# Scores and maxima of a grouped attention in 32-row TensorE tiles, four heads at a time

## The chip, the cores and the metric

The kernel runs on one core of a Trainium2 chip. The metric is device time in microseconds of one execution. Before the change three executions took 1123.99, 1124.51 and 1124.54; the median is 1124.51. A profile is one more execution, recorded instruction by instruction.

The engines that matter: TensorE (PE in the profile; its weight loads are shown as PEld), VectorE (DVE), ScalarE (ACT), GpSimd (POOL), and SyncE (SP), from whose queue nearly all DMAs are issued. Each engine works through its own instructions in the written order.

## The reference

One layer norm feeds two branches, and both are added to the input:

```python
xn = _layernorm(x)                        # x: 1 x 2048 x 448
# A: 16 heads of 28, one shared k and v
q = (xn @ wq) split into 16 heads; k = xn @ wk; v = xn @ wv      # 28 wide
p = softmax(q k^T * 28**-0.5, over the 2048 keys)
a = concat_heads(p v) @ wo
# B: a dense MLP
h = max(xn @ w1, 0)                       # 448 -> 1792
return x + a + h @ w2                     # 1792 -> 448
```

All data is float32.

## The kernel before, in words

**Precision.** A float32 value is split into a high part (rounded to the format float32r, which TensorE streams in one pass) and a low part, the rest. A product is then hi x hi + hi x lo + lo x hi; the scores also take lo x lo. Plain float32 matmuls, used for PV, appear in the profile as two instructions each.

**Stages.** The projection stage normalizes and transposes x in four blocks of 512 rows (`transposed`), projects q, k and v (`qkv_proj`, `qkv_first`), splits the result into both parts and writes it to a scratch in DRAM, `qscr` (`qkv_out`, L237). Then `kst` is read back (L309): a stack of 4 x 28 = 112 rows with the k parts, so that one matmul over 112 rows makes all four products of the parts. The MLP follows: 7 parts of the hidden width x 4 row blocks = 28 tasks, each with two up tiles (`mlp_up`, `proj`, 11 matmuls each, L168 and L173) and four down tiles (`mlp_down`, 6 matmuls each, L404). Last comes attention, in 16 units (4 query blocks of 512 x 4 groups of 4 heads).

**Maxima.** A softmax needs the maximum over the keys per query first. `max_tile` (L350, L354) multiplies 128 queries of one head by 512 keys and reduces the result on VectorE; 64 such tiles make a unit, 1024 in all. 192 of them run in the MLP's last 16 tasks, one between a few MLP matmuls (`LEAD, PER = 192, 12`), the other 832 in attention. `max_rows` transposes a unit's maxima (L371) and writes them by DMA into two more rows of the unit's query stack `qst`, against two rows of ones in `kst`: a score matmul over 114 rows so yields score minus maximum.

**Attention.** `score` (L628) multiplies one key block of 128 keys by 512 queries of one head and takes the exponential on ScalarE (L630). `pv` (L474) adds four heads' p by v into one PSUM bank: each head writes 32 of the 128 output rows, so four matmuls sit side by side in four column strips of TensorE. A column of ones in `vtile` gives the sums for the division. `dens`, `recips` and `normalized` divide, partly by way of DRAM; `o_proj` (L529) multiplies by wo, 12 matmuls for 128 rows; `o_proj_part` and `finish` deal with the last units.

**Order.** The order of the attention stage is written out in a string, one letter an instruction: `S` or `s` a score (PSUM pool A or M), `M` a maximum, `F` an output projection, `Vn` the PV of the oldest n key blocks. It holds 1024 scores, 832 maxima, 15 projections and 80 V groups of two to five blocks. A stretch of it:

```python
        7SM MS 2SM S V2 SSM 2MS 5SM MS 2SM S V4 2SM SSM 4MS SMMS 5SM S V4 S 3SM 2MS 5SM S V3 2SM SSM 3MS
```

PSUM has eight banks: pool A three, pool M four, pool O one. SP's queue holds, in the written order, the q writes, the loads of k and v and of the query stacks, the maxima's rows and the division's small transfers.

Of the kernel before, what the change touches and what calls it, by code (L numbers as in the profile page):

```python
# [15 lines left out]

@with_exitstack
def attention_plus_mlp(ctx: ExitStack, tc: tile.TileContext, x, wq, wk, wv, wo, w1, w2, out):
# [6 lines left out]
    NT = S // P  # L29
    QB = 512  # L30
    NQB = S // QB
    TPB = QB // P
    HG = 4
    NHG = H // HG
    NKB = S // P
# [4 lines left out]
    NPART = DFF // FP  # L40
# [5 lines left out]
    KQ = 4 * DH  # L46
    NU = NQB * NHG
    NA, NM = 3, 4
    assert DR == 64 and KQ + 2 <= P and HG * 32 == P and NPART * FP == DFF

# [4 lines left out]
    psA = ctx.enter_context(tc.tile_pool(name="psA", bufs=NA, space=PSUM))  # L55
    psM = ctx.enter_context(tc.tile_pool(name="psM", bufs=NM, space=PSUM))
    psO = ctx.enter_context(tc.tile_pool(name="psO", bufs=1, space=PSUM))

# [3 lines left out]
    for t in range(TPB):  # L62
        (nc.scalar if t % 2 else nc.sync).dma_start(acc[:, t, :], xv[:, t, :])

    ident = cst.tile([P, P], F32, name="ident")
    make_identity(nc, ident)
    vtile = cst.tile([P, NKB, 32], F32, name="vtile")
    nc.gpsimd.memset(vtile, 1.0)
    ones2 = cst.tile([2, QB], F32, name="ones2")
    nc.gpsimd.memset(ones2, 1.0)  # L70
    eps_t = cst.tile([P, 1], F32, name="eps_t")
    nc.vector.memset(eps_t, EPS)
    warm = cst.tile([P, 1], F32, name="warm")

# [3 lines left out]
    kst = cst.tile([P, S], F32R, name="kst")  # L78
    qscr = dram.tile([NHG, 2, P, S], F32, name="qscr")
    rscr = dram.tile([NU, HG, QB], F32, name="rscr")  # L80
    stacks = ctx.enter_context(tc.tile_pool(name="stacks", bufs=3))


    mlp = ExitStack()
    spool = mlp.enter_context(tc.tile_pool(name="spool", bufs=2))
    wpool = mlp.enter_context(tc.tile_pool(name="wpool", bufs=2))
    xpool = mlp.enter_context(tc.tile_pool(name="xpool", bufs=1))
    hpool = mlp.enter_context(tc.tile_pool(name="hpool", bufs=2))
    proj_scope = ExitStack()
    npool = proj_scope.enter_context(tc.tile_pool(name="npool", bufs=1, side="right"))  # L90
# [13 lines left out]
    DHH = DH // 2  # L104
    MQ = HG * DH
# [7 lines left out]
    wqkv = wpool.tile([P, 2, 4, 512], F32R, name="w")  # L113
    w4 = wqkv.rearrange("p s c (g n) -> p s c g n", g=NHG)
    nc.gpsimd.memset(w4[:, :, :, :, MQ + DHH : P].bitcast(F32), 0.0)
# [3 lines left out]
    def wqkv_parts(c, kv):  # L119
        src = (kvs if kv else s3)[:, c].rearrange("p (g n) -> p g n", g=NHG)  # L120
        cols = slice(MQ, MQ + DHH) if kv else slice(0, MQ)
        return src, w4[:, 0, c, :, cols], w4[:, 1, c, :, cols]
# [32 lines left out]
    xH = xpool.tile([P, DC, S], F32R, name="xH")  # L155
    xL = xpool.tile([P, DC, S], F32R, name="xL")
    xR = xpool.tile([P, S], F32R, name="xR")
    kstF = kst.bitcast(F32)

    def proj(ps, lhs, cols, xs, between=None, middle=None):  # L160

        n = 0
        for ws, xm in (((0, 1), xH), ((0,), xL)):
            if middle and xm is xL:
                middle()
            for c in range(DC):
                for wi in ws:
                    nc.tensor.matmul(ps, lhs[:, wi, c, cols], xm[:, c, xs], start=n == 0, stop=False)  # L168
                    n += 1
                    if between and n % 4 == 0:  # L170
                        between()
        for wi in range(2):
            nc.tensor.matmul(ps, lhs[:, wi, DC, cols], xR[:, xs], start=False, stop=wi == 1)  # L173
# [12 lines left out]

# [12 lines left out]

# [17 lines left out]
    def transposed(b, xn, chunks=range(DC + 1), order=range(TPB)):  # L217
        xs = slice(b * QB, (b + 1) * QB)
        for c in chunks:
# [3 lines left out]
            if c < DC:  # L223
                nc.scalar.activation(xH[:, c, xs], pt, AF.Copy)
                nc.vector.tensor_tensor(xL[:, c, xs], pt, xH[:, c, xs].bitcast(F32), op=ALU.subtract)
            else:
                tmp = small.tile([P, QB], F32R, name="tmp")
                nc.scalar.activation(xR[0:DR, xs], pt[0:DR], AF.Copy)
                nc.scalar.activation(tmp[DR:P], pt[DR:P], AF.Copy)
                nc.vector.tensor_tensor(xR[DR:P, xs], pt[DR:P], tmp[DR:P].bitcast(F32), op=ALU.subtract)  # L230
# [7 lines left out]

    def qkv_proj(b, g, spare=False, middle=None):
        pq = psO.tile([P, QB], F32, name="o") if spare else psA.tile([P, QB], F32, name="a")  # L240
        proj(pq, wqkv, slice(g * P, (g + 1) * P), slice(b * QB, (b + 1) * QB), middle=middle)
        return pq

    def qkv_first(gs):

        pq = [psA.tile([P, QB], F32, name="a") for _ in gs]
        passes = [(0, xH, c) for c in range(DC)] + [(0, xL, c) for c in range(DC)] + [(0, None, DC)]
        passes += [(1, xH, c) for c in range(DC)] + [(1, None, DC)]
        for n, (wi, xm, c) in enumerate(passes):
            for k, g in enumerate(gs):  # L250
                rhs = xR[:, 0:QB] if xm is None else xm[:, c, 0:QB]
                nc.tensor.matmul(  # L252
                    pq[k], wqkv[:, wi, c, g * P : (g + 1) * P], rhs, start=n == 0, stop=n == len(passes) - 1
                )
        return pq

# [18 lines left out]


# [8 lines left out]
    qkv_out(0, 3, pq)  # L285
    for b in range(1, NQB):
# [15 lines left out]
    proj_scope.close()  # L302
    stacks2 = ctx.enter_context(tc.tile_pool(name="stacks2", bufs=2, side="right"))


    for g in range(2):
        for r in range(4):
            d0 = r * DH + g * DHH
            nc.sync.dma_start(kstF[d0 : d0 + DHH, :], qscr[g, r // 2, MQ : MQ + DHH])  # L309
    for b in range(NQB):  # L310
        nc.sync.dma_start(kstF[KQ : KQ + 2, b * QB : (b + 1) * QB], ones2)
    vT = []
    for s in range(2):
        t = stacks.tile([P, HG, QB], F32, name="qst")
        vT.append(t.rearrange("d j q -> d (j q)")[0:DH])
        for g in range(2):
            nc.sync.dma_start(vT[s][g * DHH : (g + 1) * DHH], qscr[2 + g, s, MQ : MQ + DHH])
    nc.gpsimd.tensor_tensor(vT[0], vT[0], vT[1], op=ALU.add)

    def v_rows():  # L320

        pv = psM.tile([P, QB], F32, name="m")
        for kb in range(NKB):
            nc.tensor.transpose(pv[:, kb * 32 : kb * 32 + DH], vT[0][:, kb * P : (kb + 1) * P], ident[0:DH, 0:DH])
        nc.vector.tensor_copy(vtile[:, :, 0:DH], pv.rearrange("p (i d) -> p i d", d=32)[:, :, 0:DH])


    qst, nmx, mx_todo = {}, {}, []
    units = [(b, g) for b in range(NQB) for g in range(NHG)]

    def load_stack(u):
        if u >= NU:
# [355 lines left out]
```

## Time and profile before

| what | value |
|---|---|
| median of 3 executions | 1124.51 us (1123.99 to 1124.54) |
| the profiled execution: span, first to last instruction | 1122.0 us |
| its own time | not recorded beside the span; the median is 2.5 us above the span |
| projections, MLP, attention with its ending | 59.1, 321.8, 741.1 us |
| matmul instructions | 5900 |

A row of a group names the line, the engine, the operation, output and inputs with their shapes and the count; then the busy time of all of them in microseconds and the mean of one in nanoseconds; then how long the engine had been idle just before them, and what ended that. Matmuls overlap, so the mean of one is longer than the distance between two. In a row in order of time the first number is the start and the second the length, of one instruction or of a run of like ones ("x16"). In a stretch (A:B) each engine's busy time is followed by its number of instructions; at the end stand the granted TensorE clock, the DMA share and GB/s.

### The profile page before, as it was taken

Reading aid. Unit: us, or ns where it says so; the run is one execution under the profiler, and the core shown is the slowest. Engines: PE = TensorE matmul, PEld = TensorE weight load, DVE = VectorE, ACT = ScalarE, POOL = GpSimd, SP = SyncE. Lnnn points to the kernel's source line nnn. Section 1 sums busy time; section 2 is a strip of 40 time slices with the busy share of each in tenths; the row PEclk is TensorE's granted clock in tenths of the full one; section 3 lists DMA queues with packets and bytes.
Section 4 is the critical chain, followed back from the end, with each engine's and each line's share of the span. In section 5 each row is a group of like instructions: output and inputs, shape, how many; then the busy total and the mean of one; then the engine's idle time right before and its main releaser. Section 6 shows DMA issues by size and latency. Waiting matters only on the chain.

```text
span 1122.0 us, 15424 instructions
## 1 busy us (share of the span) xinstructions
PE 1116.4 (99%) x5900; PEld 743.6 (66%) x5900; DVE 791.9 (71%) x1383; ACT 588.5 (52%) x1173; POOL 115.9 (10%) x100
## 2 busy tenths in 40 slices
PE   9999999999999999999999999999999999999998
PEld 8888888888888755555656555556565555656555
DVE  7634337888888878778876878876877877777602
ACT  5511110011000467767866767766766777666894
POOL 3232022020200101010010101101011010010110
PEclk9999999999999999999999999999999999999999
DMA  7781610001000101011012020111101100000001
GB/s 242 259 175 39 144 36 1 1 1 37 1 1 1 30 1 44 12 33 44 15 30 59 11 52 2 44 24 37 43 18 44 33 12 11 18 11 10 11 11 41
DMA packets 34432, 45.95 MB, mean 41 GB/s; under 512 B 10056, under 2 KB 21000, under 8 KB 34192
## 3 DMA queue, kind: packets, MB, share of 16 engines
q1 hardware_dynamic: 34072, 44.52, 15.1%
q8 instruction: 46, 0.75, 0.3%
q10 hardware_dynamic: 288, 0.46, 0.1%
q14 instruction: 26, 0.21, 0.1%
HBM read 32.37 MB, written 12.18 MB: 40 GB/s over the span
## 4 chain that ended last, share of the span: by engine, by line
PE 99%; DVE 0%; DMA 0%; issue 0%; ACT 0%
PE a L628 22%; PE m L350 22%; PE o L474 21%; PE a L168 12%; PE a L404 9%; PE o L404 3%; PE a L173 3%; PE m L529 3%; PE m L628 1%; PE m L550 1%; PE a L252 1%; PE m L222 1%; DMA acc<-in_A_x 0%; PE a L588 0%; DVE st L181 0%; PE o L168 0%
## 5 line engine op out<-in xcount | busy, mean ns | idle before, releaser
L354 DVE TENSOR_REDUCE nmx<-m 128x1 f32<-128x512 f32 x1024 | 633.0, 681 | 151.5 <-PE m L350 151.1
L630 ACT ACTIVATE p<-a 128x512 f32<-128x512 f32 x974 | 495.0, 638 | 163.9 <-PE a L628 163.2
L350 PE MATMUL m<-kst,qst 112*128 112x512 f32 x1024 | 393.4, 400 | 0.0
L628 PE MATMUL a<-qst,kst 114*128 114x512 f32 x974 | 379.5, 413 | 0.0
L628 PEld LDWEIGHTS a<-qst,kst 114*128 114x128 f32 x974 | 182.9, 188 | 139.6 <-ACT p L630 63.6
L474 PE MATMUL o<-p,vtile 128*32 128x512 f32 x2048 | 236.3, 596 | 0.0
L350 PEld LDWEIGHTS m<-kst,qst 112*128 112x128 f32 x1024 | 193.5, 189 | 42.1 <-DVE nmx L354 12.5
L391 ACT ACTIVATE hH<-a 128x512 fp32r<-128x512 f32 x56 | 33.5, 599 | 266.0 <-PE a L173 143.0
L474 PEld LDWEIGHTS o<-p,vtile 128*32 128x32 f32 x2048 | 58.5, 109 | 127.2 <-issue 123.0
L168 PE MATMUL a<-xH,w 128*128 128x512 f32 x408 | 110.0, 392 | 0.0
L404 PE MATMUL a<-w,hH 128*128 128x448 f32 x336 | 96.0, 367 | 0.0
L392 DVE SCALAR_TENSOR_TENSOR hL<-a,hH 128x512 fp32r<-128x512 f32 x56 | 38.7, 692 | 69.7 <-ACT hH L391 69.7
L168 PEld LDWEIGHTS a<-xH,w 128*128 128x128 f32 x408 | 76.7, 188 | 15.8
L515 POOL TENSOR_TENSOR on<-rb,oS 128x512 f32<-128x512 f32 x15 | 19.3, 1289 | 643.9 <-DMA rb<-rscr 512.6
L404 PEld LDWEIGHTS a<-w,hH 128*128 128x128 f32 x336 | 63.6, 189 | 8.6
L168 PE MATMUL a<-xL,w 128*128 128x512 f32 x204 | 63.1, 392 | 0.0
L411 DVE TENSOR_TENSOR acc<-a,acc 128x448 f32<-128x448 f32 x84 | 51.8, 617 | 14.8 <-PE a L404 14.8
L404 PE MATMUL a<-w,hL 128*128 128x448 f32 x168 | 61.4, 365 | 0.0
L168 PEld LDWEIGHTS a<-xL,w 128*128 128x128 f32 x204 | 38.2, 188 | 8.2
L173 PE MATMUL a<-xR,w 128*128 128x512 f32 x136 | 41.9, 389 | 0.0
L404 PEld LDWEIGHTS a<-w,hL 128*128 128x128 f32 x168 | 31.6, 188 | 2.5
L404 PE MATMUL o<-w,hH 128*128 128x448 f32 x112 | 32.0, 367 | 0.0
(119 smaller groups left out, 536.9 us busy)
## 6 DMA issues: line engine op xcount, KB each, us to landing
qst<-qscr SPq DMA_DIRECT2D x64, 224.0 KB
qscr<-qs SPq DMA_DIRECT2D x16, 512.0 KB
rb<-rscr SPq DMA_DIRECT2D x60, 64.0 KB
out<-acc SPq DMA_DIRECT2D x16, 224.0 KB
acc<-in_A_x SPq DMA_DIRECT2D x14, 224.0 KB
stg<-in_B_w SPq DMA_DIRECT2D x7, 448.0 KB
stg<-in_B_w SPq DMA_DIRECT2D x7, 384.0 KB
d<-oS SPq DMA_DIRECT2D x60, 2.0 KB
```

The source lines that it names most:

```text
L168: nc.tensor.matmul(ps, lhs[:, wi, c, cols], xm[:, c, xs], start=n == 0, stop=False)
L173: nc.tensor.matmul(ps, lhs[:, wi, DC, cols], xR[:, xs], start=False, stop=wi == 1)
L350: nc.tensor.matmul(pm, qst[u][0:KQ, j, s * P : (s + 1) * P], kst[0:KQ, k0 : k0 + QB], start=True, stop=True)
L354: nc.vector.tensor_reduce(nmx[u][:, n, h : h + 1], pm, axis=AX.X, op=ALU.max)
L391: nc.scalar.activation(hH[:, f], ph, AF.Relu)
L392: nc.vector.scalar_tensor_tensor(hL[:, f], ph, 0.0, hH[:, f].bitcast(F32), op0=ALU.max, op1=ALU.subtract)
L404: nc.tensor.matmul(py[:, 0:D], hm[:, f, i * P : (i + 1) * P], wd[:, wi, f, :], start=n == 0, stop=n == 3 * FC - 1)
L411: nc.vector.tensor_tensor(acc[:, t, :], py[:, 0:D], acc[:, t, :], op=ALU.add)
L474: nc.tensor.matmul(o_acc[u][32 * j : 32 * j + 32], vtile[:, kb, :], p, start=kb == 0, stop=kb == NKB - 1)
L529: nc.tensor.matmul(py[:, 0:D], om[:, i * P : (i + 1) * P], wm[:, g, :], start=n == 0, stop=n == 3 * NHG - 1)
L628: nc.tensor.matmul(pt, kst[0 : KQ + 2, kb * P : (kb + 1) * P], st, start=True, stop=True)
L630: nc.scalar.activation(p, pt, AF.Exp, scale=SCALE)
```

## The change

**Row tiles.** The 112-row stack goes. A head's 28 rows, and two for the maximum, lie in one strip of 32 partitions, four heads of a group in the four strips. k is kept four times, once in each strip, as high part (`kH`) and low part (`kL`, with ones in the two extra rows). A score is three matmuls of 28, 28 and 30 rows in one strip into one bank: k hi x q hi, k hi x q lo, k lo and ones x q hi and minus maximum (lo x lo is dropped). A maximum is one matmul of 28 rows, hi x hi. Four heads are issued strip by strip, each into its own bank.

```diff
-    kst = cst.tile([P, S], F32R, name="kst")
+    kH = cst.tile([P, S], F32R, name="kH")
+    kL = cst.tile([P, S], F32R, name="kL")
...
-        pm = psM.tile([P, QB], F32, name="m")
-            pm, qst[u][0:KQ, j, s * P : (s + 1) * P], kst[0:KQ, k0 : k0 + QB], start=True, stop=True
+        pm = bank(b)
+        rows = slice(RB * r, RB * r + DH)
+            pm, qhi[u][rows, s * P : (s + 1) * P], kH[rows, h * QB : (h + 1) * QB], start=True, stop=True
...
+    def burst(style, banks):
+        u, kb = divmod(n_s, NKB)
+        n_max = len(banks) - HG
+        heads = [todo[i][1] for i in range(n_max)]
+        seq = []
+        for r in range(HG):
+            m = ["M"] * heads.count(r)
+            seq.append(m + [0, 1, 2] if style == "b" else [0, 1, 2] + m)
+        keys = slice(kb * P, (kb + 1) * P)
+        for i in range(max(map(len, seq))):
+            for r in range(HG):
+                if i >= len(seq[r]):
+                    continue
+                k = seq[r][i]
+                if k == "M":
+                    max_mm(banks.pop(0), r)
+                    continue
+                if k == 0:
+                    ps[r] = bank(banks.pop(0))
+                w, s, m = ((kH, 0, DH), (kH, 1, DH), (kL, 0, DH + 2))[k]
+                rows = slice(RB * r, RB * r + m)
+                nc.tensor.matmul(ps[r], w[rows, keys], qst[u][rows, s, :], start=k == 0, stop=k == 2)
+                if k == 2:
+                    p = ppool.tile([P, QB], F32, name="p")
+                    nc.scalar.activation(p, ps[r], AF.Exp, scale=SCALE)
+                    ptile[n_s][r] = p
```

**Loads.** k is read back from the scratch block by block while the projections still run, 16 DMAs a block on SP's queue, in front of the block's last q write. After the last block come three loads of queries' high parts for the maxima (`load_qhi`), 16 loads of v, and three full query loads (`load_q`: both parts in one DMA).

```diff
+    def load_k(b):
+        xs = slice(b * QB, (b + 1) * QB)
+        for s, dst in ((0, kH), (1, kL)):
+            for g, n in kparts:
+                src = qscr[g, s].rearrange("(j d) q -> j d q", d=RB)[0 : n // KV, DH:RB, xs]
+                for j in range(HG):
+                    d0 = j * RB + g * HG * KV
+                    nc.sync.dma_start(dst.bitcast(F32)[d0 : d0 + n, xs], src)
...
     for b in range(1, NQB):
...
         qkv_out(b, 2, qkv_proj(b, 2))
+        load_k(b)
...
+    for u in range(3):
+        load_qhi(u)
```

**Order.** One string now orders the MLP and attention, with the PSUM bank of each step (eight banks, named; bank 7 is PV's). `Fn,b` starts the next MLP tile in bank b and does n of its matmuls, `fn` does n more; `M2647` are four maxima into these banks; `Bb052643` is a key block's burst of four scores, with one maximum for each bank over four (before the scores in style b, after them in style a); `V1` is the PV of one key block; `R1` a unit's row maxima; `r`, `n` the division's steps; `On,b` an output projection.

```diff
+    F11,0 M12345 F11,6 F3,7 M0123 f8 F3,4 f3 M5601237 f5 F6,5 F6,6 F6,0 F6,1 M2374 v5601 F3,2 M0315 f8
...
+    M23 V1 Bb052643 M1 V1 Bb50261 M43 V1 Bb50423 M61 V1 Bb256041 M3 V1 Bb62053 M41 V1 Bb26401 M53 V1
```

Counted from the string: the MLP part has 168 tiles and 361 maxima in 70 bursts of four to seven. If the strips of a burst run side by side and a strip's own steps one after another, these are 107 rounds. Attention has 256 bursts (155 with one maximum in style b, 58 with two, 24 in style a without any, 19 others), 310 maxima in bursts and 353 as words of their own between a burst and the next V. 239 of the 245 V words take one block; PV of a block comes after the next block's burst. In rounds, with a strip's steps between two other words counted together, attention's 3735 tiled matmuls are 1008 rounds, in 258 separate spells. No maxima are left for the last unit or so, as before.

**What stays.** The projections' and the MLP's matmuls in number and shape, PV's matmuls, the division, the output projection in 12 steps (9 for the last block without its last unit), the ending, 24 buffers for p.

More of the change, by code (lines that the diff above doesn't have):

```diff
@@ L152, in split_part, with proj_steps @@
         )
[L155 to L173, printed above, removed]
+    xT = {}
+    def proj_steps(lhs, xt):
+        steps = [(lhs(wi, c), xt[:, c]) for c in range(DC) for wi in range(2)]
+        steps += [(lhs(0, c), xt[:, DC + c]) for c in range(DC)]
+        return steps + [(lhs(wi, DC), xt[:, 2 * DC]) for wi in range(2)]
     stat = {}
@@ L318, in attention_plus_mlp @@
[L318 to L332, printed above, removed]
-            return
-        b, g = units[u]
-        st = (stacks if u % 5 < 3 else stacks2).tile([P, HG, QB], F32R, name="qst")
-        qst[u] = st
-        for r in range(4):
-            src = qscr[g, r % 2, 0:MQ, b * QB : (b + 1) * QB].rearrange("(j d) q -> d j q", d=DH)
-            nc.sync.dma_start(st.bitcast(F32)[r * DH : (r + 1) * DH], src)
@@ L471, in pv @@
+    o_acc, o_sb, o_r, o_hl = {}, {}, {}, {}
+    EQ = QB * HG // P
+    n_v = 0
+    late = {}
+    def pv():
+        nonlocal n_v
+        u, kb = divmod(n_v, NKB)
         if kb == 0:
[L472 to L473 removed]
+            o_acc[u] = psB.tile([P, QB], F32, name="o")
+        ps = ptile.pop(n_v)
+        n_v += 1
+        for j in range(HG):
             nc.tensor.matmul(
[L475 removed]
+                o_acc[u][RB * j : RB * (j + 1)], vtile[:, kb, :], ps[j], start=kb == 0, stop=kb == NKB - 1
```

594 lines of the change are left out of this document (312 added, 282 removed).

## The prediction

> **What bounds the kernel now.** I read the page from the top first (span, busy times, slices), then the groups, then stretches cut at the stage borders, and last single stretches in order of time for prices.
>
> ```profile
> span 1122.0 us, 15424 instructions
> PE 1116.4 (99%) x5900; PEld 743.6 (66%) x5900; DVE 791.9 (71%) x1383; ACT 588.5 (52%) x1173; POOL 115.9 (10%) x100
> ...
> L354 DVE TENSOR_REDUCE nmx<-m 128x1 f32<-128x512 f32 x1024 | 633.0, 681 | 151.5 <-PE m L350 151.1
> L630 ACT ACTIVATE p<-a 128x512 f32<-128x512 f32 x974 | 495.0, 638 | 163.9 <-PE a L628 163.2
> L350 PE MATMUL m<-kst,qst 112*128 112x512 f32 x1024 | 393.4, 400 | 0.0
> L628 PE MATMUL a<-qst,kst 114*128 114x512 f32 x974 | 379.5, 413 | 0.0
> L474 PE MATMUL o<-p,vtile 128*32 128x512 f32 x2048 | 236.3, 596 | 0.0
> ```
>
> TensorE is never idle; VectorE and ScalarE wait mostly for it (the 151.1 and 163.2 at the ends of their rows). So TensorE time is the currency, and the floors behind it are VectorE's 791.9 and ScalarE's 588.5. The stages, in stretches (columns: time, then busy time and instructions of each engine):
>
> ```profile
> 0.00:59.10 59.10, 57.12 (x300) 48.92 (x301) 40.10 (x99) 30.37 (x58) 17.96 (x35) 1.00 0.73 247
> 59.10:380.90 321.80, 321.80 (x1490) 277.98 (x1488) 220.93 (x369) 34.08 (x58) 41.42 (x13) 1.00 0.16 36
> 380.90:1113.00 732.10, 732.10 (x4094) 413.64 (x4093) 526.24 (x902) 523.48 (x1055) 55.43 (x48) 1.00 0.10 25
> 1113.00:1122.00 9.00, 5.34 (x23) 3.02 (x21) 4.64 (x13) 0.60 (x4) 1.09 (x4) 0.92 0.35 127
> ```
>
> Projections take 59.1, the MLP 321.8, attention 741.1 with its ending. The prices come from three places in order of time: a run of alternating score and maximum matmuls, a PV group, and a single ScalarE stretch.
>
> ```profile
> 601.96 0.39 PE L628 MATMUL a<-qst,kst 114*128 114x512 f32 x1
> 602.15 4.28 DVE L354 TENSOR_REDUCE nmx<-m 128x1 f32<-128x512 f32 x7 [3.65 <-PE m L350]
> ...
> 605.70 0.40 PE L628 MATMUL a<-qst,kst 114*128 114x512 f32 x1
> ...
> 611.25 0.39 PE L628 MATMUL a<-qst,kst 114*128 114x512 f32 x1
> 611.57 0.16 PEld L474 LDWEIGHTS o<-p,vtile 128*32 128x32 f32 x8 [0.36 <-issue]
> 611.57 2.78 PE L474 MATMUL o<-p,vtile 128*32 128x512 f32 x24
> 614.28 0.19 PEld L628 LDWEIGHTS a<-qst,kst 114*128 114x128 f32 x1 [0.84 <-issue]
> 614.39 0.19 PEld L350 LDWEIGHTS m<-kst,qst 112*128 112x128 f32 x1
> 614.62 0.40 PE L350 MATMUL m<-kst,qst 112*128 112x512 f32 x1
> ```
>
> Sixteen matmuls lie between 601.96 and 605.70: 0.234 a step of 512 columns. From the end of the last step before PV (611.25 + 0.234) to the start of the first after it (614.62 - 0.234) are 2.90 for 24 PV instructions, three key blocks. A group of one block more takes 0.86 longer in the chain below (2.71 against 3.57), so a key block of PV is 0.86 and going into the column tiles and out again 0.32. Seven reductions in 4.28, the last 0.68 long: 0.60 each. An exponential runs every 0.48, from 1058.57 to 1060.48 four of them:
>
> ```profile
> 69.16 2.43 PE a L404 x12
> 79.04 2.43 PE a L404 x12
> ...
> 414.30 2.71 PE o L474 x24
> 500.74 3.57 PE o L474 x32
> 606.11 2.48 PE m L529 x12
> ...
> 1058.57 0.70 ACT L630 ACTIVATE p<-a 128x512 f32<-128x512 f32 x1
> 1060.48 0.75 ACT L630 ACTIVATE p<-a 128x512 f32<-128x512 f32 x1
> ```
>
> An output-projection step is 2.48/12 = 0.207. An MLP task (two up tiles, four down tiles) without maxima repeats after 79.04 - 69.16 = 9.88. These prices rebuild the time before: MLP 28 x 9.88 + 192 x 0.234 = 321.6 (321.8 seen); attention (1024 + 832) x 0.234 + 256 x 0.86 + 80 groups x 0.32 + 180 x 0.207 + 9 for the ending = 726 (741 seen; 15, or 2%, is what the sum misses).
>
> **The change, part by part.** *Projections.* The same matmuls in another column layout; 59.1 stays. What changes is SP's queue. A block's 16 loads of k rows go in ahead of the q writes of the next block, 64 in all, where eight and four tiny ones came at the end.
>
> ```profile
> 20.70 1.81 SPq L237 DMA_DIRECT2D qscr<-qs  x3
> 29.30 29.20 SPq L237 DMA_DIRECT2D qscr<-qs  x13
> 58.59 3.83 SPq L309 DMA_DIRECT2D kst<-qscr  x8
> ...
> 1081.09 0.34 SPq L507 DMA_DIRECT2D rscr<-r  x1
> 1082.54 1.70 SPq L510 DMA_DIRECT2D rb<-rscr  x4
> 1086.01 1.29 POOL L515 TENSOR_TENSOR on<-rb,oS 128x512 f32<-128x512 f32 x1 [30.49 <-DMA rb<-rscr]
> ```
>
> A k load costs SP 3.83/8 = 0.48, a q write 1.81/3 = 0.60. From 29.3 on: 13 writes 7.8, four groups of loads 30.7; a read behind a write waits 1.1 (1082.54 - 1081.43), four times 4; then the first query tile, 0.4 and 1.8 to its use (1086.01 - 1084.24). That is about 74, while TensorE has its first up tile done at 61.6 and the next word of the order is a maximum that needs those queries. Everything behind it on TensorE waits, MLP too. Bounds 0 (a block's SP work, 7.7 + 2.4, is no more than its four projections of 11 steps of 0.23, so SP may keep up) and 14; I take 12. The v loads and full query loads queue behind it, but are first read some 20 later.
>
> *MLP.* 361 maxima in place of 192, in 70 bursts, counted from the order text. Four heads' maxima in four row strips are one round if they overlap; the bursts hold 107 rounds. TensorE: 28 x 9.88 = 276.6, 107 x 0.234 = 25.0, and 70 changes of tiling. The trace of before has one spell in 32-row tiles, the 16 small transposes of v:
>
> ```profile
> 105.63 0.61 PE L173 MATMUL a<-xR,w 128*128 128x512 f32 x2
> 106.17 1.06 PEld L324 LDWEIGHTS m<-ident,qst 28*128 28x128 f32 x16 [0.35 <-issue]
> 107.78 0.37 PE L404 MATMUL a<-w,hL 128*128 128x448 f32 x1
> ...
> L324 PEld LDWEIGHTS m<-ident,qst 28*128 28x128 f32 x16 | 1.1, 137 | 0.4 <-issue 0.4
> L222 PEld LDWEIGHTS m<-ident,hH 128*128 128x128 f32 x32 | 4.1, 141 | 1.4 <-DVE hH L210 1.0
> L392 DVE SCALAR_TENSOR_TENSOR hL<-a,hH 128x512 fp32r<-128x512 f32 x56 | 38.7, 692 | 69.7 <-ACT hH L391 69.7
> L411 DVE TENSOR_TENSOR acc<-a,acc 128x448 f32<-128x448 f32 x84 | 51.8, 617 | 14.8 <-PE a L404 14.8
> ```
>
> The second L173 step ends at 105.63 + 2 x 0.234 = 106.10. The matmul at 107.78 is the third of its kind at 0.203, so the first began at 107.37. Between lie 1.27, of which 16 steps at (1.06 - 0.137)/15 = 0.0615 are 0.98: about 0.3 for in and out, as for the column tiles. So 70 x 0.32 = 22.4, together 324. VectorE in this stage: 361 x 0.60 + 56 x 0.69 + 112 x 0.617 = 324 as well. Two engines at par lose a little to each other; I add 8 (0 to 20).
>
> *Attention, TensorE.* Scores become three 28- or 30-row steps per head (k hi x q hi, k lo x q hi with the query's other half, see the diff) instead of one 112-row step: 3072 steps. The 663 maxima left are one step each. Laid out by strip, with each strip working through its own list between two PV groups, the order gives 3735 steps in 1008 rounds, most key blocks having four. At 0.234: 235.9. PV is unchanged: 256 x 0.86 = 220.2. But PV now comes one key block at a time: 258 changes of tiling x 0.32 = 82.6, 57 more than before. Output projection 180 x 0.207 = 37.2, 13 row transposes 4, the ending 9. Sum 589.
>
> *Attention, the others.* A key block is then about 2.11 of TensorE (4 x 0.234 + 0.86 + 0.32), against 4 x 0.48 = 1.91 of ScalarE and 2.6 x 0.60 = 1.6 of VectorE. Before, PV ran two to five blocks behind; now one. A strip's last step begins 0.47 after the block's start; its record lasts 0.40, so the first exponential can begin near 0.9, and the fourth ends at 0.9 + 3 x 0.48 + 0.64 = 3.0 (mean of an exponential 638 ns). PV of the block is due at 2.11 + 0.94 + 0.09 = 3.14, a margin of 0.1. The seven banks are as tight: 4 scores and 2.6 maxima a block. The queue is in order: what waits for p or for a bank holds back the next scores, and with them the next exponential. Every delay of ScalarE is therefore TensorE's. Bounds 0 and 61 (a cycle of 2.35, the margin gone and a bank late each time); I take 0.09 a block, 23, somewhat more than the 15 that the sum missed before.
>
> *Small edits*, at nothing: the full queries come in one load a unit in place of four, and a second load brings their upper halves, 0.5 of SP each, hidden under a unit of 30 and more; the row maxima go out in four writes in place of two, a unit or more before their scores; the fills of k and v tiles lie on POOL (115.9 busy of 1122), the copies of v on ScalarE, which the MLP leaves idle. Without that cover they cost a microsecond or two each, once.
>
> *The unshown price* is that four row strips work at once, loads included. The nearest rows: PV's four column strips do (2048 instructions of 596 ns are 1221 in 236.3 of busy time, and eight loads of 110 ns start within 0.16 - 0.11 = 0.05). Lower bound of a step: 0.234/4 = 0.0585. L324 steps, one strip alone, 0.0615: hardly more. Upper bound with overlapping streams: loads one at a time, 0.11 each, the distance of the loads at 614.28 and 614.39. Without any overlap 0.234. I take 0.0585, for PV is the only row with tiles side by side.
>
> **Sum.** 59.1 + 12 + 324 + 8 + 589 + 23 = 1015 of span. The profiled execution has span 1122.0; the median 1124.51 is 2.5 above it, which I carry: **1018 us**, 9.5% under before.
>
> **Rivals.** *Loads one at a time (slower).* In column tiles each strip may have its own way in; row strips share columns. A load of 28 rows is no shorter than one of 128 (137 against 141 ns above), so tiling makes four loads of one. At 0.11 a step attention needs 3735 x 0.11 = 411, 175 more, the MLP 361 x 0.11 = 40, 15 more; the 23 of coupling vanish in the longer cycle: 1018 + 175 + 15 - 23 = 1185. The same price results if a strip's own load isn't hidden under its own stream (0.19 + 0.234 = 0.42 a round). It decides above 0.095 a step, where the 4096 tiled steps have eaten the gain of 106 and the 23. Against it stand PV's loads.
> The Trainium skill, in TensorE: Matmul & The Clock Gate, section LDWEIGHTS (loading the stationary operand), has the load time go by columns and not by rows; the two rows agree, and by it alone, without overlap of loads, the result is this rival's.
>
> *Rounds stretched by a third.* Strips overlap but start staggered, each step costing 0.076, a round 0.305: 1008 x 0.071 + 107 x 0.071 = 79 more, 1097. Nothing in the rows before shows such a stagger, nor excludes it between 0.0585 and 0.11.
> The same page, Part 3: Packing small matmuls, section Measured speedup vs the span model, measured 3.07 times, not 4, for four row tiles of 512 columns; no run here shows it yet, and 4 x 0.234/3.07 is this round.
>
> *ScalarE and banks couple.* A cycle of 2.35: 61 in place of 23, 1056. For it speaks the margin of 0.1 worked out above; against it, that 7 banks hold the 6.6 of a block, and that ScalarE has 0.2 of slack in a cycle of 2.11.
>
> *No row overlap at all*, that is, the change doesn't do what it says: (3735 x 0.234 - 236) + (361 x 0.234 - 25) = 697 more, some 1690. PV speaks against it.
>
> **How the numbers follow.** Forecast case 0.57 (its own range 965 to 1045: no SP wait, no imbalance and no coupling make 975, cheaper tiling changes some 10 less), coupling 0.09, stretched 0.10, within 0.2% 0.02, loads one at a time 0.17, no overlap 0.03, another wait that I don't see, slower, 0.02. Faster 0.76, same 0.02, slower 0.22; 0.2% is about what a measurement of this kernel can tell from no change. The range must hold eight in ten: 965 to 1150 takes in the first four cases, and of the loads case the part with steps of 0.10 (about 1145).
>
> **What would show it.** Right: a burst's four steps start within some tens of ns and a round lasts 0.234; TensorE loads in a burst lie on top of each other; attention begins near 403 and lasts about 612; TensorE's idle time near 62 to 74 ended by the query DMA. Wrong: loads 0.1 apart in the bursts; a key block of 2.7 instead of 2.2; waits of TensorE for p or for banks of more than 0.1 a block; ScalarE back to back in attention; VectorE ending the MLP.

## The result and the profile after

The changed kernel takes 1063.19 us (median of four executions, 1061.46 to 1064.91), against 1124.37 for the kernel before: a ratio of 0.946, with a 95% interval of 0.944 to 0.947. 1018 was forecast, with a range of 965 to 1150. The direction and the mechanism held; 45 us of the expected gain did not come. The changed kernel and the four kernels of the next section ran four times each; every other kernel below ran once, so a difference of a few microseconds between those says nothing.

The page of the changed kernel: span, busy time of the engines, and the groups that answer to those shown of before (here a group's row names the line, the shapes, busy time, mean of one, and the idle time before it).

```profile
span 1062.9 us, 20180 instructions
PE 1024.6 (96%) x7948; PEld 604.8 (57%) x7948; DVE 810.3 (76%) x1382; ACT 601.0 (57%) x1177; POOL 114.9 (11%) x101
...
L434 DVE TENSOR_REDUCE nmx<-b 128x1 f32<-128x512 f32 x980 | 628.2, 684 | 130.7 <-PE b L431 108.7
L492 ACT ACTIVATE p<-b 128x512 f32<-128x512 f32 x1024 | 528.0, 615 | 91.2 <-PE b L489 80.7
L431 PE MATMUL b<-kH,qhi 28*128 28x512 f32 x980 | 268.5, 465 | 14.2 <-DMA q<-qscr 13.4
```

There are 2048 more matmuls than before (7948 against 5900), and TensorE's time still falls by 92. TensorE remains the busy engine, but it now has idle time, and the longest piece is a wait of 13.4 for a DMA in the row of the maxima (L431).

The stretches, cut at the new stage borders (time, then busy time and instructions of TensorE, its loads, VectorE, ScalarE, GpSimd; at the end granted clock, DMA share, GB/s):

```profile
0.00:59.10 59.10, 51.42 (x265) 43.81 (x266) 36.86 (x94) 25.86 (x51) 19.64 (x35) 0.94 0.60 191
59.10:97.00 37.90, 12.98 (x36) 9.37 (x35) 4.15 (x6) 4.96 (x8) 0.95 (x1) 0.68 0.48 167
97.00:110.00 13.00, 12.98 (x51) 9.22 (x52) 8.50 (x14) 1.21 (x3) 0.25 (x1) 0.76 0.30 91
110.00:430.20 320.20, 319.11 (x1608) 245.54 (x1606) 306.86 (x528) 33.08 (x60) 37.81 (x13) 1.00 0.09 25
430.20:1054.00 623.80, 622.82 (x5973) 293.75 (x5972) 449.11 (x729) 535.54 (x1055) 55.15 (x48) 0.99 0.10 28
1054.00:1062.90 8.90, 5.25 (x22) 3.07 (x21) 4.80 (x13) 0.39 (x3) 1.08 (x4) 0.98 0.28 103
```

The span is 1062.9 where the sum had 1015, 48 more. They fall into three pieces. The first maximum runs at 97.0, not near 73.6: 23.4. From there to attention are 333.2, not 329.5: 3.7. Attention with its ending is 632.7, not 612: 20.7. So there are two things to explain: the wait ahead of the MLP, and some 20 us in attention. First the part that came out as priced, a key block in order of time:

```profile
484.85 0.18 PEld L489 LDWEIGHTS b<-q,kH 28*128 28x128 f32 x1 [0.84 <-issue]
484.86 0.49 PE L489 MATMUL b<-q,kH 28*128 28x512 f32 x1
484.86 0.18 PEld L431 LDWEIGHTS b<-kH,qhi 28*128 28x128 f32 x1
484.86 0.49 PE L431 MATMUL b<-kH,qhi 28*128 28x512 f32 x1
484.86 0.30 PEld L489 LDWEIGHTS b<-q,kH 28*128 28x128 f32 x6
...
485.99 0.16 PEld L558 LDWEIGHTS o<-p,vtile 128*32 128x32 f32 x8 [0.37 <-issue]
485.99 1.07 PE L558 MATMUL o<-p,vtile 128*32 128x512 f32 x8
...
486.99 0.50 PE L489 MATMUL b<-q,kH 28*128 28x512 f32 x3
```

The four strips' first loads and matmuls lie on top of each other: they start within 10 ns. Fourteen tiled steps, four rounds, take 1.13 from 484.86 to 485.99; PV takes 1.00, and the block repeats after 2.13. The sum had 4 x 0.234 + 0.32 + 0.86 = 2.12. That a round costs no more than one step shows apart from the change of tiling too: between two PVs, the spells of 12 steps, three rounds, have a median of 0.92, those of 14 steps, four rounds, 1.13.

### The profile page after: what moved, and what is told of

The parts are those of the page before. It is cut to its first block, busy times and chain, and to the rows that moved or that the text cites. A ratio compares the mean times of both kernels' runs of the same rounds, so it can differ in the third digit from the quotient of the medians.

```text
span 1062.9 us, 20180 instructions
## 1 busy us (share of the span) xinstructions
PE 1024.6 (96%) x7948; PEld 604.8 (57%) x7948; DVE 810.3 (76%) x1382; ACT 601.0 (57%) x1177; POOL 114.9 (11%) x101
## 4 chain that ended last, share of the span: by engine, by line
PE 88%; SPq 5%; DMA 3%; DVE 2%; ACT 1%; issue 1%; ACTq 0%; DVEq 0%
PE o L558 24%; PE b L489 23%; PE b L521 11%; PE b L535 11%; PE b L431 9%; SPq L285 4%; PE b L598 4%; PE o L521 3%; DMA qscr<-qs 1%; PE o L535 1%; DVE nmx L434 1%; DMA stg<-in_B_w 1%; DMA stg<-in_A_wq 0%; DVE acc L541 0%; PE o L431 0%
## 5 line engine op out<-in xcount | busy, mean ns | idle before, releaser
L434 DVE TENSOR_REDUCE nmx<-b 128x1 f32<-128x512 f32 x980 | 628.2, 684 | 130.7 <-PE b L431 108.7
L492 ACT ACTIVATE p<-b 128x512 f32<-128x512 f32 x1024 | 528.0, 615 | 91.2 <-PE b L489 80.7
L431 PE MATMUL b<-kH,qhi 28*128 28x512 f32 x980 | 268.5, 465 | 14.2 <-DMA q<-qscr 13.4
L489 PE MATMUL b<-q,kH 28*128 28x512 f32 x2048 | 260.6, 441 | 0.1
L489 PEld LDWEIGHTS b<-q,kH 28*128 28x128 f32 x2048 | 134.7, 183 | 164.2 <-DVE nmx L434 93.8
L431 PEld LDWEIGHTS b<-kH,qhi 28*128 28x128 f32 x980 | 119.8, 183 | 102.5 <-DVE nmx L434 49.9
L489 PE MATMUL b<-q,kL 30*128 30x512 f32 x1024 | 170.6, 395 | 0.6 <-DMA q<-rows 0.6
L521 PE MATMUL b<-xt,w 128*128 128x512 f32 x495 | 129.3, 408 | 8.1 <-DVE qs L291 7.9
L535 PE MATMUL b<-w,hH 128*128 128x448 f32 x408 | 118.3, 371 | 0.1
L489 PEld LDWEIGHTS b<-q,kL 30*128 30x128 f32 x1024 | 98.4, 184 | 9.5 <-DMA q<-rows 1.8
```

The lines of the kernel that those rows point to most:

```text
L431: nc.tensor.matmul(pm, qhi[u][rows, s * P : (s + 1) * P], kH[rows, h * QB : (h + 1) * QB], start=True, stop=True)
L434: nc.vector.tensor_reduce(nmx[u][:, r, s, h : h + 1], pm, axis=AX.X, op=ALU.max)
L489: nc.tensor.matmul(ps[r], w[rows, keys], qst[u][rows, s, :], start=k == 0, stop=k == 2)
L492: nc.scalar.activation(p, ps[r], AF.Exp, scale=SCALE)
L521: nc.tensor.matmul(ph, w, xm, start=i == 0, stop=i == len(steps) - 1)
L535: nc.tensor.matmul(py[:, 0:D], hm[:, i * P : (i + 1) * P], wm, start=k == 0, stop=k == len(steps) - 1)
```

## Experiments on the wait ahead of the MLP

SP's queue of the changed kernel in order of time (L285 the k loads, L292 the q writes, L380 and L396 the loads of queries and of v):

```profile
29.40 0.37 SPq L292 DMA_DIRECT2D qscr<-qs  x1
29.82 7.76 SPq L285 DMA_DIRECT2D kH<-qscr  x8
37.69 5.60 SPq L285 DMA_DIRECT2D kL<-qscr  x8
43.39 1.81 SPq L292 DMA_DIRECT2D qscr<-qs  x3
46.73 5.70 SPq L285 DMA_DIRECT2D kH<-qscr  x8
52.47 6.03 SPq L285 DMA_DIRECT2D kL<-qscr  x8
58.60 3.14 SPq L292 DMA_DIRECT2D qscr<-qs  x4
63.02 5.88 SPq L285 DMA_DIRECT2D kH<-qscr  x8
68.94 5.59 SPq L285 DMA_DIRECT2D kL<-qscr  x8
74.63 3.08 SPq L292 DMA_DIRECT2D qscr<-qs  x4
78.98 5.94 SPq L285 DMA_DIRECT2D kH<-qscr  x8
84.96 5.59 SPq L285 DMA_DIRECT2D kL<-qscr  x8
90.65 0.37 SPq L292 DMA_DIRECT2D qscr<-qs  x1
93.52 1.29 SPq L380 DMA_DIRECT2D qhi<-qscr  x3
```

Sixteen k loads take 5.88 + 5.59 = 11.5 of SP, 0.72 each, where the sum took the 0.48 of the old kernel's k loads. The four groups take 48.3 in all and not 30.7; 2 of this are waits in the first group, until two loads of weights have landed. And each group stands still until a q write before it has landed. Such a write takes 2.85 to 3.92 from its issue to its landing, but SP issues two more writes meanwhile (before the queries' loads it issues none), so it stands still for 1.5, 1.3, 1.3 and 2.5 (45.20 to 46.73, 61.74 to 63.02, 77.71 to 78.98, 91.02 to 93.52), 6.6 where 4.4 were taken. The 13 writes take 8.8 and not 7.8, and from the first query load to the first maximum are 3.5 and not 2.2. So the loads are 17.6 more, the waits 2.2, the writes 1.0 and the end 1.3: 22 of the 23.4. The price of a load is nearly all of it.

TensorE does not meet this as one wait. It stands still four times, together 30.4: 5.50 at 48.15, 3.67 at 63.24, 7.90 at 79.20 and 13.37 at 97.02.

```profile
63.24 8.06 PE L303 MATMUL a<-xt,w 128*128 128x512 f32 x22 [3.67 <-DVE qs L291]
...
77.74 0.60 ACT L290 ACTIVATE qs<-a 128x512 fp32r<-128x512 f32 x1 [8.80 <-DMA qscr<-qs]
...
79.20 4.45 PE L521 MATMUL b<-xt,w 128*128 128x512 f32 x11 [7.90 <-DVE qs L291]
...
97.02 1.19 PE L431 MATMUL b<-kH,qhi 28*128 28x512 f32 x5 [13.37 <-DMA q<-qscr]
```

The first three are in the projections and at the MLP's first up tile: the split of a projection (ScalarE L290, then VectorE L291) waits for one of four staging buffers `qs`, which come free when a q write has landed, and SP issues these writes late. The projections so end at 71.3 and not at 59.1. The row of 97.02 names `q<-qscr`, a load of v of which a piece came in last; the load of the queries, issued at 93.52, has landed at 96.72, just before.

What the idle engine costs afterwards is seen in order of time: 11 steps of the next up tile take 5.06, 0.43 a step, and not 0.234.

```profile
98.14 5.06 PE L521 MATMUL b<-xt,w 128*128 128x512 f32 x11
```

The granted clock of 97 to 110 is 0.76 in the stretches above. The Trainium skill, TensorE: Matmul & The Clock Gate, section Why this matters for your kernels, has it that an idle gap of TensorE beyond some 3 us brings the clock back to half; here gaps of 7.9 and 13.4 do, so the trace agrees. At 0.76 these 13 us lose 3.1, most of the MLP's 3.7.

**Fewer, larger k loads.** In k_once a DMA reads a group's k rows for all 2048 keys at once: 16 loads, after the last block's k is written, in place of 64. In k_once_split only the high parts go in ahead of the queries.

```diff
-        load_k(b)                        # 16 DMAs a block, 512 keys each
+        if last:
+            load_k(((0, kH), (1, kL)))   # 16 DMAs, 2048 keys each
```

> Edit: k is read back from the scratch once, all 2048 columns in 16 DMAs after the last block, in place of 16 DMAs behind each of the four blocks. Theory A (SP's queue): 64 loads of 0.72 and the waits for the q writes before them keep SP busy until 94 and the first maximum until 97.0. With 16 loads SP gets there near 73, the first maximum starts near 77, and the time falls by about 20, to 1043. Theory B (the bytes and the landing of the last k rows decide, not the queue): longer rows land no earlier, the first maximum stays near 97 and the time near 1063.

> Edit: as k read once, but only the high part of k, which the maxima need, goes in front of the last q write and the queries; the low part follows the queries. Theory A: eight loads less in front of the queries, 8 x 0.72 = 6 earlier than with all sixteen: first maximum near 71, time near 1037. Theory B: as after the change, near 1063.

They take 1050.69 us (ratio 0.936 [0.934, 0.938]) and 1048.06 (0.932 [0.931, 0.934]). The first maximum comes at 85.0 and 75.0, where 77 and 71 were expected. The queue of k_once shows why 85 and not 77:

```profile
62.52 8.46 SPq L285 DMA_DIRECT2D kL<-qscr  x8
71.59 0.38 SPq L292 DMA_DIRECT2D qscr<-qs  x1
81.52 1.28 SPq L380 DMA_DIRECT2D qhi<-qscr  x3
```

The query loads wait from 72.0 to 81.5 for that one q write, because `qhi` lies in the memory from which it is sent. From issue to landing such a write took under 4 us before; here, behind 16 loads of long rows, it takes 9.9, and in k_once_split, behind eight, 9.0. In k_once_split part of the time won goes into the next wait: TensorE stands 4.91 at 98.1 for GpSimd's sum of the v parts, whose loads have moved back on SP. So fewer loads do bring the first maximum forward, by 12 in k_once; the landing of a write took back part of it, and a third wait was hidden behind both.

**Queries ahead of k.** queries_first adds a buffer of its own for `qhi`, so that it need not wait for the q staging, loads the queries ahead of the high parts of k, the low parts behind v, and moves the use of v (`v5601`) back by nine MLP tiles. k_hi_early besides reads the high parts of three blocks as soon as these are written, while the last block is projected.

```diff
+    hipool = ctx.enter_context(tc.tile_pool(name="hipool", bufs=3, side="right"))
...
+        if last:
+            for u in range(3):
+                load_qhi(u)
+            load_k(((0, kH),), NQB - 1)
...
+        if b == NQB - 2:
+            load_k(((0, kH),), 0, NQB - 1)
```

> Edit: as k read once with its low part later, and the three loads of queries for the maxima stand ahead of the k loads, in a pool of their own, so that they need not wait until the last q write has landed; the low part of k follows v, and v is turned into rows some 25 later. Theory A (the first maximum waits for SP's queue and for that write): first maximum near 66, then the MLP's 332 and attention's 631 as they are: time near 1031. Theory B (landing of the k rows behind all other transfers decides): first maximum stays at 75, time at 1040 or more.

> Edit: as queries first, but the high part of k is read in two goes: the first three blocks' columns behind the third block's last q write, the last block's 512 columns where all of them were read. The first twelve maxima need only the first three blocks. Theory A (the eight k loads and their landing, 58 to 73 in queries first, are the last thing that the first maxima wait for): first maximum near 62 and no halting behind it, time 10 to 12 less, near 1030. Theory B (the loads in the middle delay the q writes of the last block by as much): within 4 of 1041.

queries_first takes 1041.16 (0.926 [0.925, 0.928]): its first maximum runs at 69.1, but the maxima halt until 73.6 for pieces of k, so the time is not the 1031 that was hoped for. k_hi_early takes **1033.48 us** (1033.21 to 1034.72), a ratio of 0.920 [0.918, 0.921], the best kernel of this study. Its start of the MLP in order of time:

```profile
57.47 2.84 SPq L297 DMA_DIRECT2D qhi<-qscr  x3
...
62.24 5.66 SPq L286 DMA_DIRECT2D kH<-qscr  x8
...
64.91 1.21 PE L437 MATMUL b<-kH,qhi 28*128 28x512 f32 x5 [3.92 <-DMA qhi<-qscr]
...
68.01 0.39 SPq L304 DMA_DIRECT2D qscr<-qs  x1
```

The first maximum stands at 64.9, 32.1 earlier than in the changed kernel, and the span is 1031.4, 31.5 shorter: the wait was worth nearly its full length, for the stages behind it keep theirs: the MLP 334.5, attention with its ending 632.0.

## Experiments on the row tiles themselves

**Order within a burst.** The changed kernel issues step 0 of the four strips, then step 1 of the four, and so on. strips_in_turn issues a strip's steps together, then the next strip's.

```diff
-        for i in range(max(map(len, seq))):
-            for r in range(HG):
-                if i >= len(seq[r]):
-                    continue
-                k = seq[r][i]
+        for r in range(HG):
+            for k in seq[r]:
```

> Edit: the steps of a burst are issued strip after strip in place of round by round; the same 14 or 15 steps and the same banks in number. Theory A (the strips overlap, and it is the interleaved issue that makes them): a strip's steps follow one another and only the last of one lies beside the first of the next, so a burst takes 10 rounds of 0.234 instead of 4, some 2.3 in place of 1.33; attention grows by about 230, to 1290. Theory B (a tiled step costs its 0.06 wherever it stands in the order): no change beyond 20.

It takes 1109.64, 46 more and not some 230: the expectation was wrong. One of its bursts, in order of time:

```profile
1023.09 0.49 PE L431 MATMUL b<-kH,qhi 28*128 28x512 f32 x1
1023.11 0.94 PE L486 MATMUL b<-q,kH 28*128 28x512 f32 x8
1023.67 0.61 PE L486 MATMUL b<-q,kL 30*128 30x512 f32 x4
```

In the written order a strip's kL step stands ahead of the next strip's two kH steps. By the trace all eight kH steps start before the first kL step: the four strips run side by side whatever the order, so a step overtakes the steps of another strip that were written ahead of it. That an engine works through its instructions in the written order so holds for TensorE only within a strip. The Trainium skill, TensorE: Matmul & The Clock Gate, Part 3, section The mechanism, says that matmuls start and end in program order, without exception; across row strips this trace disagrees. What the 46 are, the spells between two PVs tell (from the starts of the matmuls): those of 15 steps take 1.52 in the mean in place of 1.32, 157 times, those of 14 steps 1.31 in place of 1.14, 54 times, together 41. The banks of the string then fall to other steps of a burst than they were laid out for; that these come free later was not shown by itself.

**One strip.** All tiled steps of one_strip read rows 0 to 31, with the same number of steps, rows and columns; so heads two to four of a group get the first one's scores and maxima.

```diff
-                rows = slice(RB * r, RB * r + m)
+                rows = slice(0, m)
```

> Edit: all tiled steps, of scores and of maxima, read the strip of the first head, so heads two to four of each group get the first head's scores; the steps, banks and order are the same in number. Theory A (strips overlap): in one strip 14 or 15 steps take 0.234 each in place of four rounds, 3735 x 0.234 - 236 = 638 more in attention and up to 60 in the MLP, some 1700 to 1760. Theory B (the gain comes from shorter steps or fewer passes and not from overlap): within 20 of 1063.

It takes 2655.04. Its stretches and its steps (columns as above):

```profile
430.00:1000.00 570.00, 569.02 (x1631) 340.44 (x1631) 160.15 (x260) 138.46 (x260) 16.71 (x12) 0.55 0.03 8
1000.00:2000.00 1000.00, 1000.00 (x2765) 584.19 (x2765) 238.93 (x378) 253.02 (x478) 22.10 (x21) 0.52 0.03 10
```

A spell of 15 steps now takes 6.69 (median), 15 x 0.427 (half the clock) and 0.29; the shortest takes 3.67, 15 x 0.234 and 0.16 for the change of tiling. So a strip's steps do run one after another, 0.234 each at the full clock, and with the 1.13 for four rounds above, a round of four strips takes no longer than one step alone: side by side they are worth four times. Not expected was the rest: TensorE is busy for 1000.00 of 1000 us and yet is granted 0.52 of its clock, and PV, which is unchanged, takes 1.87 and not 1.00. In this run one strip of 32 rows at work was not enough to keep the full clock.

## Experiments on the missing 20 us of attention

The spells of tiled steps between two PVs tell where they are. From the starts of the changed kernel's matmuls: 54 spells of 14 steps (four scores, two maxima) have a median of 1.13; 157 spells of 15 steps (four scores, three maxima) a median of 1.34 and a minimum of 1.13. Both are four rounds. With PV's 1.00 the block with three maxima is 2.34, the 2.35 of the rival in which ScalarE and the banks couple. 157 x 0.2 are 31. One of them, in order of time:

```profile
544.00 0.72 PE L489 MATMUL b<-q,kH 28*128 28x512 f32 x6
...
544.79 0.39 PE L489 MATMUL b<-q,kL 30*128 30x512 f32 x1
544.80 0.65 PE L431 MATMUL b<-kH,qhi 28*128 28x512 f32 x2
544.95 0.18 PEld L431 LDWEIGHTS b<-kH,qhi 28*128 28x128 f32 x1 [0.20 <-ACT p L492]
545.38 0.16 PEld L558 LDWEIGHTS o<-p,vtile 128*32 128x32 f32 x8 [0.24 <-issue]
```

The last maximum's load starts 0.20 late, released by an exponential: its bank held a score of the block before. Four scores and three maxima take all seven banks, so each bank must come back within one block. On the other side ScalarE waits for the late scores:

```profile
510.06 2.06 ACT L492 ACTIVATE p<-b 128x512 f32<-128x512 f32 x4 [0.18 <-PE b L489]
512.52 2.07 ACT L492 ACTIVATE p<-b 128x512 f32<-128x512 f32 x4 [0.39 <-PE b L489]
```

Neither engine is full, and each waits for the other. Three theories were held against this: the banks come back late from their readers; PV's wait for p, one block behind, is what couples; or a fifth round is a matter of TensorE itself.

**Distance of PV, and of the banks.** pv_lag2 leaves out the first `V1`, so that PV runs two blocks behind; the division's `r` and `n` move behind the next V. pv_pairs takes two blocks in each V. max_after_pv puts the separate maxima behind V.

```diff
 changed       Ba6120 Bb543641 M23 V1 Bb052643 M1 V1 Bb50261 M43 V1
+pv_lag2       Ba6120 Bb543641 M23 Bb052643 M1 V1 Bb50261 M43 V1
+pv_pairs      Ba6120 Bb543641 M23 Bb052643 M1 V2 Bb50261 M43 Bb50423 M61 V2
+max_after_pv  Ba6120 Bb543641 M23 V1 Bb052643 V1 M1 Bb50261 V1 M43
```

> Edit: PV runs two key blocks behind the scores in place of one, with the division's steps moved along. Theory A (PV waits for the exponentials of the block just done): 20 to 25 less, time near 1040. Theory B (banks, not p, are what is waited for): time within 8 of 1063.

> Edit: PV of two key blocks at a time wherever no division step stands between, some 120 groups less, so two bursts follow each other. By the price of 0.33 for a change of tiling alone: 40 less, 1023. By the banks: the second burst needs four banks for scores while ScalarE needs 1.9 to give back the first four, so TensorE waits about 1 in each pair, which a PV between them had filled: 80 more, near 1140.

> Edit: the maxima that stand between a key block's burst and the next PV are issued after this PV, so they begin the next spell in the row tiles. Theory A (these maxima wait for banks that ScalarE has not given back, and hold up PV behind them): spells of 15 steps fall from 1.32 to about 1.2, attention by 25 to 30, time near 1036. Theory B (whatever is taken away there comes back as a wait at the next burst, because ScalarE sets the pace): time within 8 of 1063.

pv_lag2 takes 1089.67. Its 15-step spells stay at a median of 1.35, so the wait for p is not the cause. The time was expected near 1040 or 1063; 14 of the 26 more are idle time of TensorE, 5.8 at the longest, and the rest was not traced. pv_pairs takes 1162.85, where 1023 or, by the banks, 1140 was expected: it saves half of the changes of tiling (16 PV matmuls in 1.85, not 2 x 1.00), but a spell of 30 steps takes 3.60 (median) where eight rounds and a change would be about 2.1: two blocks need 14 banks and there are seven. max_after_pv takes 1317.04, where nothing above 1071 was expected: a separate maximum then has its bank named again in the very next burst, ahead of any PV (`M1 Bb50261`), and spells of 15 steps take 2.76 (median). So the two kernels in which a bank's name returns sooner are slower by much, and the one that keeps this distance keeps its spells.

**The readers of the banks.** half_reduce lets VectorE's reduction in attention take 256 of the 512 keys; exp_three_quarters lets ScalarE take 384 of the 512 queries, while GpSimd fills the rest of p; half_readers halves both, with fixed p buffers whose second half is filled once.

```diff
+            nmx[u][:, r, s, h : h + 1], pm if ppool is None else pm[:, 0 : QB // 2], axis=AX.X, op=ALU.max
...
+                    p = pfix[(HG * n_s + r) % P_BUFS]
+                    c = QB // 2
+                    nc.scalar.activation(p[:, 0:c], ps[r][:, 0:c], AF.Exp, scale=SCALE)
```

> Edit: in attention a maximum is reduced over the first 256 of its 512 keys; the other half is left out, so VectorE gives a bank back about 0.27 earlier. Theory A (the 0.2 by which a burst of 15 steps exceeds its four rounds are waits for banks that VectorE holds): bursts fall from 1.33 to 1.2 or less, time from 1063 to about 1030. Theory B (ScalarE holds them, one key block of lag being too little): bursts stay near 1.33, time within 8 of 1063.

> Edit: the exponential is taken over 384 of the 512 queries, GpSimd fills the other 128 columns with a constant; these are left out of the result. ScalarE then needs about 0.37 in place of 0.48 for each. Theory A (a third maximum in a key block waits for a bank in which ScalarE still reads the block before): spells of 15 steps fall from 1.32 to 1.2 or less, time from 1063 to about 1035. Theory B (neither VectorE nor ScalarE, but TensorE's own order of steps makes the fifth round): spells of 15 steps stay near 1.32, time within 8 of 1063.

> Both readers of attention's banks do half the work: VectorE's reduction takes 256 of the 512 keys of a maximum, ScalarE's exponential 256 of the 512 queries (left out: the other half of both; the other half of the 24 p buffers is filled once with a constant, so that PV streams what it did before). TensorE's instructions and the names of the banks stay. In the changed kernel 157 key blocks have 15 tiled steps between two PVs, which take 1.34 (median) where four rounds and a change would be 1.13, and 239 of 849 steps that start late there start 30 to 60 ns behind the end of an exponential, 118 behind the end of a reduction. Theory (banks come back late from both readers, so halving one of them alone, as for VectorE, shows nothing): the 15-step spells fall to 1.13 to 1.18, 157 x 0.19 = 30 less, 1033 us (1028 to 1042). Rival (the fifth round is TensorE's own, 15 steps over four strips): they stay at 1.3, and the time at 1055 to 1063.

half_reduce takes 1060.70 and its 15-step spells 1.35 (median); exp_three_quarters 1103.76 and 1.35. In the latter TensorE got a new wait of 71.5 us in all for GpSimd's fills, so its time tells nothing of the banks. half_readers takes 1026.64, 1.4 below the range that was expected, and here the spells of 15 steps fall to 1.14 (median; 1.22 at most), 178.5 us in all in place of 207.2. Attention of half_reduce, then of half_readers:

```profile
430.00:1050.00 620.00, 619.14 (x5966) 286.47 (x5961) 279.08 (x728) 535.62 (x1056) 54.48 (x48) 1.00 0.10 28
```

```profile
430.20:1014.00 583.80, 583.36 (x5952) 249.55 (x5947) 278.14 (x727) 320.96 (x1052) 54.48 (x48) 1.00 0.10 30
```

VectorE's busy time is the same in both (279 and 278), ScalarE's falls from 536 to 321, and the stage with its ending, from its first score, from 1058.6 - 429.2 = 629.4 to 1024.8 - 429.3 = 595.5 (632.7 in the changed kernel). Of these 37, 28.7 are the 157 spells and 7 the other tiled spells. TensorE's instructions are the same, so the fifth round isn't TensorE's own: it is the time until a bank has been read. Which reader it is, the weight loads of such spells tell that start more than 40 ns behind the one ahead of them: how many start 30 to 60 ns after the end of an exponential, and how many as much after the end of a reduction.

| kernel | late loads | after an exponential | after a reduction | 15-step spell, median |
|---|---|---|---|---|
| changed | 849 | 239 | 118 | 1.34 |
| half_reduce | 755 | 248 | 4 | 1.35 |
| exp_three_quarters | 610 | 53 | 117 | 1.35 |
| half_readers | 477 | 7 | 0 | 1.14 |

An even spread would put some 50 of 849 behind exponentials. With shorter reductions those behind reductions go, with shorter exponentials most of those behind exponentials, and either alone leaves the spell as long as it was; only where both go does it come down. So both readers hold banks up, and to speed up one of them gained next to nothing here. For ScalarE alone this rests on a run with a wait of its own (the fills), and exponentials halved alone were not tried, so how much they would give stays open.

## Why the prediction was right, and where it was off

- *Four strips at once, loads included (0.0585 a step).* Right. Loads start within 10 ns, four rounds and a change of tiling take 1.13, and in one strip alone 15 steps take 3.67 at the full clock. The price rested on PV's column strips alone, since no row of before has row strips side by side and L324's steps stream only 28 columns; that it came out whole was not to be read from them. Loads one at a time (1185) and no overlap (1690) are refuted by the rows at 484.86; the round of 0.305 (1097) by 1.13 for four rounds. The 3.07 times of the Trainium skill (TensorE: Matmul & The Clock Gate, Part 3, section Measured speedup vs the span model) isn't what this trace shows: it shows four.
- *Tiling changes 0.32, PV 0.86.* Right: 1.00 + 1.13 = 2.13 against 0.86 + 0.32 + 4 x 0.234 = 2.12. Attention with its banks read in time (half_readers, 595.5) stands against the sum's 589.
- *SP's queue, 12 us (0 to 14).* The step that failed. The wait ends with the queries' DMA as was named, but it is 35 (12 + 23.4), beyond the bound. The term that was mis-sized is the k load: 0.48, from eight loads of another shape in the old kernel, was 0.72, and 64 of them 48.3 instead of 30.7. The read behind a write, 1.1 from a small transfer at the end of the kernel, was 1.3 to 2.5, which adds only 2.2. The upper bound was this sum itself and so no bound. The lower bound's reason, that SP may keep up with the projections, fell with the price of a load: 11.5 for loads, 3.1 for writes and 1.3 of waiting repeat every 16.0 (63.02 to 78.98), and a block's four projections of 11 steps take 10.3. With it fell the term "59.1 stays": the projections wait for SP by way of their staging buffers, and TensorE idles 30.4 in four pieces, not once between 62 and 74.
- *MLP, 324 + 8.* Right to 3.7, and these come with the clock after the idle gap. VectorE is the second engine at its limit, as worked out: 306.86 of 320.20.
- *Coupling, 23 (0 to 61).* The mechanism was right, the size too small: 632.7 - 595.5 = 37. It is not 0.09 in each block but next to nothing in blocks with two maxima and 0.2 in those with three. The text had both numbers, 2.35 for a block with a bank late and 7 banks for 6.6; the mean hid that most blocks use all seven. The rival (1056) named the cause, and its price, 2.35, was that of the block with three maxima; for every block it is too much.
- *Small edits at nothing.* Not quite: once SP's wait was gone, the v loads cost a wait of their own (4.91 in k_once_split).

The two misses, 23.4 and 37.2 - 23 = 14.2, with 6.5 of attention and 3.7 of the MLP, are the 48.

## What to carry to other kernels

Row strips with short contractions are worth their full factor, four here, also when each step is followed by another of its strip; price them as rounds plus about 0.33 us for each pair of changes of tiling. What they then need is banks: count them for the fullest block, not for the mean, and see that every reader of a bank, not only the slower one, is done one block later. A DMA loop that is moved in front of another stage is priced with its own shape and with the landing of the writes that it reads, since such a wait was handed on nearly in full (31.5 of 32.1); here fewer loads, and first those that the next stage needs first, gave 30 us back.

## What the runs showed of the hardware that was not expected

- Matmuls of different row strips start out of the written order: eight steps from 1023.11 on, ahead of kL steps (from 1023.67) that stand between them in the program (strips_in_turn).
- TensorE's being busy did not by itself keep the clock up: 0.52 was granted with one strip of 32 rows in the tiled steps and TensorE busy for 1000 of 1000 us (one_strip), 0.99 with four (the changed kernel).
- A DMA write of 0.38 us of issue took 9.9 us to land behind 16 loads of long rows (k_once) and 9.0 behind eight (k_once_split), and 2.85 to 3.92 behind loads of short ones (the changed kernel).
